# A planned kernel for banded attention and two MLPs: PSUM banks counted per engine, four banks for one block's h, an earlier region, other priorities

## The chip, the cores and the metric

One core of a Trainium2 chip runs the whole program. The metric is the device time of one execution in microseconds; for the kernel before it is the median of three runs. TensorE (PE) does the matrix products and transposes, VectorE (DVE), ScalarE (ACT) and GpSimd (POOL) the elementwise work, SyncE (SP) issues nearly all DMAs. PSUM, where products arrive, has eight banks here, each of 128 partitions by 512 fp32 values.

## What is computed

```python
rel = pos[:, None] - pos[None, :]
mask = (rel >= 0) & (rel < 128)
scores = np.where(mask, q @ k.T / sqrt(64) + slope[head] * -abs(rel), -1e9)
attn = softmax(scores)                       # + 1e-9 in the denominator
x = (attn @ v)                               # 4 x 576 rows = 2304 rows, 8 heads x 64 = 512 columns
h = x @ w_in                                 # 512 -> 2048
P = a[0] + a[1]*h + a[2]*h**2 + a[3]*h**3
Q = 1 + abs(b[0])*abs(h) + abs(b[1])*h**2
x = (P / (Q + 1e-6)) @ w_out                 # 2048 -> 512
h = x @ w2_in                                # the second MLP
out = (h * sigmoid(h)) @ w2_out
```

## The kernel before

Activations lie transposed, features on partitions and rows along the free dimension. Each fp32 factor is split into a high part (rounded to fp32r) and a low part (the rest), and a product is made of three fp32r matmuls: high x high, high x low and low x high.

The 18 tiles of 128 rows form five blocks (4, 4, 3, 4 and 3 tiles, `blk1`). For each block, `group` does attention for the four pairs of heads: scores (L674), a mask and maximum on VectorE (L680, L687), the exponential on ScalarE (L691), normalisation (L710 or L716), transposes (L730), the split of P into own and previous tile (L758, L760 on GpSimd, L767, L771 on VectorE), the product with V (L799) and its high and low parts xh, xl (L811).

`step` does one of the 16 slices of the first MLP's hidden dimension for a block. `mh` makes h in two halves of six matmuls (L844 to L846) in a bank of the pool h, which has two. The rational function follows in eleven operations that alternate between ScalarE (L860, L866, L877, L881, L883) and VectorE (L874, L878, L879, L885, L887, L889), of which L860, L866, L874, L878, L879, L883, L885, L887 and L889 read or write the bank of h; its temporaries t1, t2 and t3 have two buffers each (`actb`). The result's parts gh and gl (`c_hi`, `c_lo`, helpers at L447, L451, L455 for copies and L462, L466 for differences) have three. The second product `ma` (L913 to L915) adds into four banks acc0 to acc3, two and a half steps later. Two more banks, atA and atB, belong to attention, and later to the second MLP.

The second MLP works on thirds of 768 rows, each in phase A and phase B, with seven products in place of eight for a 2 x 2 split (`CHAIN`, Strassen's scheme in Winograd's form). `prep` makes the sums and differences of both weights (raw, sums, st) in DRAM while the first MLP still runs, and the products stream them back. `x_forms` makes seven forms F0 to F6 of a third's input, one buffer each, with differences xs and high and low parts; `phase_a` makes 56 products of six matmuls (L1183 to L1185) and the SiLU (L366); `phase_b` makes 56 chunks of six matmuls (L1249 to L1251), for each of which a high part xh_b and a low part xl_b, and for some a difference g, have to be there first; the rings of xh_b and xl_b hold eight chunks in all. The buffers of the forms lie where attention's lay: `open2` (L1005) closes attention's pools and opens them, and the zero-cost operation `opener` (L1012) waits for the operations in `last_att`.

The order is not written by hand. Each instruction, or bundle, is an `Op` with one or more engines that may run it, a cost in ns, its reads and writes, and a priority in units of a step. `schedule` plays the program once: of all that is ready it takes what can start first, and among those that can start within `look` ns the one with the lowest priority. Ring buffers are handed out in the order of priority. `LATENCY` is added between dependent operations on different engines; `port_free` keeps VectorE and GpSimd apart on SBUF. The order that comes out is the program's order on each engine; the waits on the chip are set by the data and by the banks. `OPT` holds the choices of engine and the leads and distances of priorities (`xlead` of `x_forms`, `hlead` and `tlead` of phase B's operands, `la` and `lb` the lengths of the phases in units, `pw2`, `rw2`, `pwo2`, `rwo2` of `prep`, `pl` of the reload of a partial sum). `SHIFTS` adds an amount to the priorities of runs of operations.

Of the kernel before, what the change touches and what calls it, by code (L numbers as in the profile page):

```python
# [21 lines left out]
P = 128  # L22
# [6 lines left out]
MASK_FAR = 2.56e11  # L29

# [5 lines left out]
    'gh': 'act|dve|pool',  # L36
    'gl': 'pool',
    'whi': 'act',
    'wlo': 'pool',
# [10 lines left out]
    'tabs': 'pool',  # L50
    'stb': 3,
    'strb': 3,
    'wpro': 1.037,
    'dS': -1.576,
    'dT': -0.149,
    'dA': 0.106,
    'dm': 0.288,
    'look': 2.453,
    'pw': -0.828,
    'pwo': -0.969,  # L60
    'dg': 0.261,
# [7 lines left out]
    'pl': 1.625,  # L69
    'qlead': 2.916,  # L70
    'keen': 9999.0,
    'norm0': 'act',
# [6 lines left out]
    'la': 8.923,  # L79
    'lb': 10.6,  # L80
    'dm2': 0.291,
    'sums': 'dve|pool',
    'fhi': 'act|pool',
# [9 lines left out]
    'tlead': 0.985,  # L93
    'hlead': 1.0,
    'oq': 'sp',
    'pw2': 35.931,
    'rw2': 2.459,
    'pwo2': 80.807,
    'rwo2': 0.657,
    'xlead': 7.017,  # L100
    'slead': 1.6,
# [14 lines left out]
]  # L116

def c_act(n, psum=False, aps=0):  # L120
# [1277 lines left out]
```

## Time and profile before

| | |
|---|---|
| median of three runs | 917.33 us (916.65 to 919.83) |
| the profiled execution, its own time | 920.78 us |
| its span, first to last instruction | 918.7 us |
| TensorE busy, share | 875.1 us, 95% |
| VectorE, ScalarE, GpSimd busy, share | 76%, 64%, 67% |
| mean granted clock of TensorE | 0.989 |
| DMA, mean | 249 GB/s, 228.94 MB |

The page gives busy times of one execution. TensorE's busy time contains the time in which a matmul stands in its queue, so the share says little alone; a stretch is read by its count of matmuls beside its length. In a table of stretches, the columns are the stretch, its length, then busy time and, in brackets, the number of instructions of TensorE, its weight loads, VectorE, ScalarE and GpSimd, then the granted clock, the DMA share and GB/s. A timeline row has start and duration in us, engine, line, operation, tile written and tiles read, shape, count, and in square brackets the idle time of the engine before it and what ended that.

### The profile page before, as it was taken

What the parts mean: (1) busy time and instruction counts of PE and PEld (TensorE: products, weight loads), DVE (VectorE), ACT (ScalarE), POOL (GpSimd) and SP (SyncE); (2) the same over time, 40 slices, a digit from 0 to 9 for tenths busy, and PEclk for the clock granted to TensorE, in tenths of its full rate; (3) what the DMA queues carried; (4) which work ended last, traced back from release to release, by engine and by line L of the source; (5) the groups of instructions that cost most, each with busy time, mean ns of one, the idle gap of its engine ahead of it and who ended that gap; (6) DMA issues with size and microseconds to landing.
All of it is one profiled execution on the core that took longest, in us unless ns stands there. A gap on an engine that the chain in (4) does not pass through costs nothing.

```text
span 918.7 us, 15313 instructions
## 1 busy us (share of the span) xinstructions
PE 875.1 (95%) x5072; PEld 769.7 (84%) x5072; DVE 700.7 (76%) x1382; ACT 583.5 (64%) x1253; POOL 618.9 (67%) x591
## 2 busy tenths in 40 slices
PE   8879899999999999999998999999999999999998
PEld 6647667877777888777777989999899998999998
DVE  5789988789999989999998985449843389533662
ACT  5878888689887788878777775336323365233441
POOL 2255655454767779778788776559954499645895
PEclk8989999999999999999999999999999999999999
DMA  7645585367798879757796888988788898788884
GB/s 238 252 133 165 197 273 165 137 199 275 234 340 260 252 243 307 243 192 239 239 345 221 286 266 303 325 296 285 239 279 256 264 307 256 250 270 253 249 269 167
DMA packets 80606, 228.94 MB, mean 249 GB/s; under 512 B 8464, under 2 KB 17168, under 8 KB 80528
## 3 DMA queue, kind: packets, MB, share of 16 engines
q1 hardware_dynamic: 78224, 219.58, 73.3%
q10 hardware_dynamic: 2304, 8.39, 2.3%
q8 instruction: 40, 0.66, 0.3%
q14 instruction: 38, 0.31, 0.1%
HBM read 178.65 MB, written 49.28 MB: 248 GB/s over the span
## 4 chain that ended last, share of the span: by engine, by line
PE 55%; DVE 15%; POOL 10%; ACT 10%; DMA 6%; issue 3%; SPq 0%; POOLq 0%; ACTq 0%; DVEq 0%
PE h L844 4%; PE z_a L1183 4%; PE z_a L1185 4%; PE z_a L1184 4%; PE h L845 3%; PE h L846 3%; POOL xf L466 3%; DVE t L874 3%; PE acc L913 3%; PE acc L915 2%; PE acc L914 2%; ACT t L866 2%; PE z_b L1249 2%; PE z_b L1251 2%; PE z_b L1250 2%
## 5 line engine op out<-in xcount | busy, mean ns | idle before, releaser
L913 PE MATMUL acc<-gh,wo 128*128 128x512 f32 (+1 forms) x320 | 121.4, 379 | 1.0 <-ACT x L447 0.8
L915 PE MATMUL acc<-gl,wo 128*128 128x512 f32 (+1 forms) x320 | 118.3, 370 | 2.7 <-POOL gl L466 2.6
L914 PE MATMUL acc<-gh,wo 128*128 128x512 f32 (+1 forms) x320 | 118.1, 369 | 0.4 <-POOL wo L466 0.4
L447 ACT CAST xh_b<-g 128x384 fp32r<-128x384 f32 x137 | 68.5, 514 | 78.7 <-PE z_b L1251 36.2
L462 DVE TENSOR_TENSOR xl_b<-g,xh_b 128x384 fp32r<-128x384 f32 x75 | 99.3, 1364 | 22.3 <-ACT xh_b L447 19.0
L466 POOL TENSOR_TENSOR gl<-t,gh 128x512 fp32r<-128x512 f32 (+1 forms) x80 | 98.5, 1231 | 22.6 <-ACT gh L447 15.6
L466 POOL TENSOR_TENSOR xl_b<-g,xh_b 128x384 fp32r<-128x384 f32 x93 | 107.6, 1172 | 3.8 <-ACT xh_b L447 1.2
L844 PE MATMUL h<-xh,ws 128*128 128x512 f32 (+1 forms) x256 | 97.0, 379 | 11.3 <-DVE t L889 11.2
L846 PE MATMUL h<-xh,ws 128*128 128x512 f32 (+1 forms) x256 | 93.0, 363 | 0.0
L845 PE MATMUL h<-xl,ws 128*128 128x512 f32 (+1 forms) x256 | 92.9, 363 | 0.0
L366 ACT ACTIVATE g<-t_a 128x384 f32<-128x384 f32 x72 | 37.8, 525 | 84.2 <-DVE t_a L359 84.2
L874 DVE SCALAR_TENSOR_TENSOR t<-t,ab,h 128x512 f32<-128x512 f32 (+1 forms) x80 | 55.3, 691 | 22.6 <-ACT t L866 20.0
L913 PEld LDWEIGHTS acc<-gh,wo 128*128 128x128 f32 x320 | 60.1, 188 | 13.8 <-issue 4.5
L915 PEld LDWEIGHTS acc<-gl,wo 128*128 128x128 f32 x320 | 60.1, 188 | 11.7 <-POOL gl L466 4.1
L844 PEld LDWEIGHTS h<-xh,ws 128*128 128x128 f32 x256 | 48.0, 188 | 25.3 <-DVE t L889 17.9
L466 POOL TENSOR_TENSOR g<-g,g 128x384 f32<-128x384 f32 x57 | 64.6, 1142 | 3.9 <-DVE xl_b L462 1.5
L914 PEld LDWEIGHTS acc<-gh,wo 128*128 128x128 f32 x320 | 60.1, 188 | 8.1 <-POOL wo L466 1.5
L860 ACT ACTIVATE t<-h,ab 128x512 f32<-128x512 f32 (+1 forms) x80 | 51.2, 641 | 23.4 <-PE h L846 22.9
L691 ACT ACTIVATE e<-e,m 128x128 f32<-128x128 f32 x144 | 56.2, 391 | 13.8 <-DVE m L687 13.5
L1183 PE MATMUL z_a<-xf,w2s 128*128 128x384 f32 x192 | 64.2, 334 | 0.4 <-DVE t L889 0.4
L1249 PE MATMUL z_b<-xh_b,wo2s 128*128 128x384 f32 x192 | 64.1, 334 | 0.0
L1251 PE MATMUL z_b<-xh_b,wo2s 128*128 128x384 f32 x192 | 64.1, 334 | 0.0
(178 smaller groups left out, 2736.1 us busy)
## 6 DMA issues: line engine op xcount, KB each, us to landing
w2s<-forms_w SPq DMA_DIRECT2D x84, 512.0 KB, 4.5
wo2s<-forms_wo SPq DMA_DIRECT2D x84, 512.0 KB, 4.6
ws<-sc SPq DMA_DIRECT2D x64, 512.0 KB, 4.8
raw_w<-in_w SPq DMA_DIRECT2D x32, 512.0 KB, 4.9
raw_wo<-in_wo SPq DMA_DIRECT2D x32, 512.0 KB, 4.6
forms_w<-st_w SPq DMA_DIRECT2D x24, 512.0 KB, 5.5
forms_wo<-st_wo SPq DMA_DIRECT2D x24, 512.0 KB, 5.3
sc<-w ACTq DMA_DIRECT2D x16, 512.0 KB, 5.6
```

Of the source, the lines that this page charges most:

```text
L462: nc.vector.tensor_tensor(out=o, in0=a, in1=b, op=op)
L466: nc.gpsimd.tensor_tensor(out=o, in0=a, in1=b, op=op)
L844: nc.tensor.matmul(o, lhsT=T[W][:, 0, c], rhs=xh, start=kt == 0, stop=False)
L845: nc.tensor.matmul(o, lhsT=T[W][:, 0, c], rhs=xl, start=False, stop=False)
L846: nc.tensor.matmul(o, lhsT=T[W][:, 1, c], rhs=xh, start=False, stop=kt == KD - 1)
L874: nc.vector.scalar_tensor_tensor(out=t("t1"), in0=t("t2"), scalar=ab[:, 0:1], in1=hp_(), op0=ALU.add, op1=ALU.mult)
L913: nc.tensor.matmul(a, lhsT=T[WO][:, 0, c], rhs=T[G1][:, :n], start=first_f, stop=False)
L914: nc.tensor.matmul(a, lhsT=T[WO][:, 1, c], rhs=T[G1][:, :n], start=False, stop=False)
L915: nc.tensor.matmul(a, lhsT=T[WO][:, 0, c], rhs=T[G2][:, :n], start=False, stop=last_f)
L1183: nc.tensor.matmul(o, lhsT=w(0, kt * P), rhs=x[:, 0, kt], start=st and kt == 0, stop=False, skip_group_check=True)
L1249: nc.tensor.matmul(o, lhsT=w(0, m * P), rhs=h, start=st and q == 0, stop=False, skip_group_check=True)
L1251: nc.tensor.matmul(o, lhsT=w(1, m * P), rhs=h, start=False, stop=q == NQ - 1, skip_group_check=True)
```

## The change

- `schedule` keeps for each PSUM bank the engine that last used it and when that ends; an operation of another engine on that bank may not start before that end plus the latency. The rule for VectorE and GpSimd on SBUF is kept by engine, with a gap of 60 ns in place of 120. A TensorE operation that starts after an idle time of over 20 ns is counted 110 ns longer, and scores and the product with V 90 ns longer, the first operation on raw weights 45 ns.
- In the last block, steps 2, 3, 6, 7, and so on take the banks atA and atB for h in place of the pool's (`tail`), so four banks go round.
- `last_att` no longer holds the operations on atA and atB.
- More engines are allowed for the parts of g and of the first MLP's weights, the table of biases, block 0's normalisation and the prepared weights' high parts; a ScalarE form of the shift of raw weights is written, and the option leaves it on VectorE. One more constant is set at the start.
- The numbers of `OPT` that set priorities are new, and so is the whole list `SHIFTS`.

```diff
-    'gh': 'act|dve|pool',
-    'gl': 'pool',
-    'whi': 'act',
-    'wlo': 'pool',
+    'gh': 'act|pool',
+    'gl': 'dve|pool',
+    'whi': 'act|pool',
+    'wlo': 'dve|pool',
...
-    'tabs': 'pool',
+    'tabs': 'act|pool',
...
-    'look': 2.453,
+    'look': 3.05,
...
-    'pl': 1.625,
-    'qlead': 2.916,
+    'pl': -6.448,
+    'qlead': 5.608,
...
-    'norm0': 'act',
+    'norm0': 'act|pool',
...
-    'la': 8.923,
-    'lb': 10.6,
-    'dm2': 0.291,
+    'la': 14.638,
+    'lb': 23.993,
+    'dm2': 0.172,
...
-    'fhi': 'act|pool',
+    'fhi': 'act|dve|pool',
...
-    'tlead': 0.985,
-    'hlead': 1.0,
+    'tlead': 1.271,
+    'hlead': -0.51,
...
-    'pw2': 35.931,
-    'rw2': 2.459,
-    'pwo2': 80.807,
-    'rwo2': 0.657,
-    'xlead': 7.017,
-    'slead': 1.6,
+    'pw2': 45.759,
+    'rw2': 6.3,
+    'pwo2': 112.144,
+    'rwo2': 0.672,
+    'xlead': 2.951,
+    'slead': 1.798,
+    'shift': 'dve',
+    'tail': 1,
...
 SHIFTS = [
...
+    (127, 57, -0.49), (282, 5, 1.3), (296, 14, 0.38), (480, 60, 0.03), (676, 69, -0.05), (787, 18, 0.2), (789, 4, -0.96), (919, 10, -0.83),
...
+PORT_GAP = 60.0
+STALL = 110.0
...
-        psum = any(t[0] in ("h", "atA", "atB") or t[0].startswith("acc") for t in list(reads) + list(writes))
-        o.port = {e for e in o.alts if e == "pool" or e == "dve" and not psum}
+        o.banks = {t[:2] for t in list(reads) + list(writes) if t[0] in ("h", "atA", "atB") or t[0].startswith("acc")}
+        o.port = {e for e in o.alts if e == "pool" or e == "dve" and not o.banks}
...
-                when = lambda o: max(f, o.ready, landed[-8] if o.dma and len(landed) >= 8 else 0.0, port_free - 120 if eng in o.port else 0.0)
+                when = lambda o: max([f, o.ready, landed[-8] if o.dma and len(landed) >= 8 else 0.0, port_free["pool" if eng == "dve" else "dve"] - PORT_GAP if eng in o.port else 0.0]
+                                     + [last_in[k][1] + LATENCY[last_in[k][0], eng] for k in o.banks if k in last_in and last_in[k][0] != eng])
...
-                o.end = free[eng] = st + o.cost
+                o.end = free[eng] = st + o.cost + (STALL if eng == "pe" and st > free.get(eng, 0.0) + 20 else 0.0)
                 if eng in o.port:
-                    port_free = o.end
+                    port_free[eng] = o.end
+                for k in o.banks:
+                    last_in[k] = (eng, o.end)
...
-            pl.op(p - 0.5, "dve", c_dve2x(NR), lambda: nc.vector.tensor_scalar(
-                out=low(), in0=low(), scalar1=29, scalar2=None, op0=ALU.logical_shift_right), reads=[rk + (0,)], writes=[rk + (0,)])
+            pl.op(p - 0.5, any_of(OPT["shift"], {
+                "act": (c_act(NR) + 45, lambda: nc.scalar.activation(out=low(), in_=low(), func=AF.Identity, scale=LOW_SCALE, bias=lnb[:, 2:3])),
+                "dve": (c_dve2x(NR), lambda: nc.vector.tensor_scalar(
+                    out=low(), in0=low(), scalar1=29, scalar2=None, op0=ALU.logical_shift_right))}), 0, None, reads=[rk + (0,), ("lnb", 0)], writes=[rk + (0,)])
...
-        Hk = ("h", g)
+        tail = OPT["tail"] and blk == nb1 - 1 and g % 4 > 1
+        Hk = (("atA", "atB")[g % 2], f"h{g}") if tail else ("h", g)
...
-                T[Hk] = h_p.tile([P, 512], F32, tag="h", name=f"h{g}")
+                T[Hk] = banks[Hk[0]] if tail else h_p.tile([P, 512], F32, tag="h", name=f"h{g}")
...
-    last_att = [o for k, l in pl.tile_ops.items() if k[0] in ("kd", "qd", "vh", "e", "ph", "m", "l", "atA", "atB", "tab", "tabs") for o in l]
+    last_att = [o for k, l in pl.tile_ops.items() if k[0] in ("kd", "qd", "vh", "e", "ph", "m", "l", "tab", "tabs") for o in l]
```

## Rows read from the trace of the kernel before

**Rows 1.** busy time, share and instructions of each engine, from the page

```profile
PE 875.1 (95%) x5072; PEld 769.7 (84%) x5072; DVE 700.7 (76%) x1382; ACT 583.5 (64%) x1253; POOL 618.9 (67%) x591
```

**Rows 2.** stretches: length, busy us and instructions by engine, clock, DMA share

```profile
35.70:471.90 436.20, 414.63 (x2413) 323.62 (x2409) 396.77 (x911) 351.14 (x768) 285.76 (x275) 0.99 0.71 233
...
471.90:551.00 79.10, 71.28 (x385) 66.44 (x385) 70.11 (x122) 61.75 (x114) 63.73 (x65) 1.00 0.81 271
...
504.90:546.20 41.30, 39.19 (x217) 37.24 (x217) 36.29 (x68) 32.77 (x62) 30.15 (x37) 1.00 0.86 281
...
612.80:676.10 63.30, 61.07 (x341) 60.10 (x340) 51.88 (x45) 30.52 (x61) 60.04 (x43) 0.97 0.84 273
676.10:733.90 57.80, 57.80 (x336) 57.80 (x335) 22.17 (x40) 18.82 (x38) 26.40 (x30) 1.00 0.83 264
```

**Rows 3.** timeline of TensorE at 469 us: start, duration, line, tiles

```profile
468.88 0.39 PE L846 MATMUL h<-xh,ws 128*128 128x512 f32 x1
469.11 0.39 PE L913 MATMUL acc<-gh,wo 128*128 128x512 f32 x1
```

**Rows 4.** waits of TensorE in the whole span: total us, times, longest

```profile
PE h L844 <- DVE t L889: 14.9, 20, 2.1
PE bank_atA L799 <- POOL ph L760: 5.3, 2, 3.2
```

**Rows 5.** waits of TensorE in 471.9:551, and who waits for L889 later

```profile
PE h L844 <- DVE t L889: 5.4, 8, 2.1
PE acc L915 <- POOL gl L466: 2.0, 1, 2.0
...
  PE z_a L1183: 0.4, 1
```

**Rows 6.** timeline in the last block, one wait and one step's h and t3

```profile
519.01 0.45 PE L844 MATMUL h<-xh,ws 128*128 128x384 f32 x1 [0.98 <-DVE t L889]
...
521.93 0.67 ACT L866 ACTIVATE t<-h,na 128x384 f32<-128x384 f32 x1
...
527.30 0.55 DVE L889 SCALAR_TENSOR_TENSOR t<-t,h 128x384 f32<-128x384 f32 x1
...
528.47 1.02 POOL L466 TENSOR_TENSOR gl<-t,gh 128x384 fp32r<-128x384 f32 x1
```

**Rows 7.** waits of VectorE in 35.7:471.9: total us, times, longest

```profile
DVE t L874 <- ACT t L866: 15.8, 28, 1.1
```

**Rows 8.** tiles w and st_wo: duration of one in ns, least, median, most

```profile
L466 POOL TENSOR_TENSOR w<-raw_w,w x16: 1290/1311/1774, 27.6 to 214.8; 128x512 fp32r<-128x512 f32 x16
...
L462 DVE TENSOR_TENSOR st_wo<-sums_wo,st_wo x4: 692/920/1490, 449.9 to 565.3; 128x512 fp32r<-128x512 f32 x4
```

**Rows 9.** groups in 612.8:676.1: count, busy us, mean ns, idle time before

```profile
L462 DVE TENSOR_TENSOR xl_b<-g,xh_b 128x384 fp32r<-128x384 f32 x28 | 38.4, 1413 | 7.8 <-ACT xh_b L447 7.8
L466 POOL TENSOR_TENSOR xl_b<-g,xh_b 128x384 fp32r<-128x384 f32 x20 | 25.7, 1305 | 0.7 <-ACT xh_b L447 0.6
...
L466 POOL TENSOR_TENSOR g<-g,g 128x384 f32<-128x384 f32 x12 | 14.2, 1196 | 0.6 <-DVE xl_b L462 0.5
...
L466 POOL TENSOR_TENSOR xf<-xf 128x768 fp32r<-128x768 f32 x3 | 6.3, 2117 | 0.1
```

**Rows 10.** timelines of GpSimd and TensorE near 660 us

```profile
656.38 2.15 POOL L466 TENSOR_TENSOR xf<-xs,xf 128x768 fp32r<-128x768 f32 x1
...
660.25 0.69 PE L1250 MATMUL bank_atA<-xl_b,wo2s 128*128 128x384 f32 x1 [2.02 <-POOL xl_b L466]
...
661.05 0.52 PE L1249 MATMUL bank_atB<-xh_b,wo2s 128*128 128x384 f32 x1
661.37 0.52 PE L1250 MATMUL bank_atB<-xl_b,wo2s 128*128 128x384 f32 x1
```

**Rows 11.** tile xl_b: duration of one in ns, least, median, most

```profile
L466 POOL TENSOR_TENSOR xl_b<-g,xh_b x93: 1004/1027/1732, 556.4 to 908.1; 128x384 fp32r<-128x384 f32 x93
L462 DVE TENSOR_TENSOR xl_b<-g,xh_b x75: 545/1364/2249, 614.7 to 901.4; 128x384 fp32r<-128x384 f32 x75
```

More of the change, by code (lines that the diff above doesn't have):

```diff
@@ L29 @@
 MASK_FAR = 2.56e11
+LOW_SCALE = 2.0 ** -29 * (1.0 - 2.0 ** -21)
 OPT = {
@@ L49 @@
     'vb': 3,
-    'tabs': 'pool',
+    'tabs': 'act|pool',
     'stb': 3,
     'strb': 3,
[L53 to L57, printed above, removed]
-    'look': 2.453,
-    'pw': -0.828,
-    'pwo': -0.969,
-    'dg': 0.261,
+    'wpro': 0.411,
+    'dS': -1.564,
+    'dT': -0.234,
+    'dA': 0.111,
+    'dm': 0.297,
+    'look': 3.05,
+    'pw': -0.803,
+    'pwo': -1.106,
+    'dg': -0.074,
     'lead': 2.526,
@@ L154 @@
 class Op:
-    __slots__ = ("eng", "cost", "fn", "alts", "prio", "deps", "ndep", "users", "start", "end", "allocs", "ready", "idx", "after", "port", "dma")
+    __slots__ = ("eng", "cost", "fn", "alts", "prio", "deps", "ndep", "users", "start", "end", "allocs", "ready", "idx", "after", "port", "dma", "banks")
 class Plan:
@@ L232, in schedule @@
         free = {}
-        port_free = 0.0
+        port_free = {"dve": 0.0, "pool": 0.0}
+        last_in = {}
         dma_free, landed = 0.0, []
@@ L477, in plan_kernel @@
         ab = const.tile([P, 2], F32, name="ab")
-        lnb = const.tile([P, 2], F32, name="lnb")
+        lnb = const.tile([P, 3], F32, name="lnb")
         tabs = tab_p.tile([P, H, 4, P], F32, name="tabs")
@@ L484, in k_ident @@
         nc.vector.memset(lnb[:, 1:2], -LN2_63)
+        nc.vector.memset(lnb[:, 2:3], 2.0 ** -18 - 0.5)
     pl.op(-99, "pool", 600, k_ident, writes=[("ident", 0), ("lnb", 0)])
@@ L540, in raw_weight @@
             low = lambda: T[rk][:, :, 0].bitcast(U32)
-            pl.op(p - 0.6, "act", c_act(NR), lambda: nc.scalar.activation(out=top(), in_=top(), func=AF.Prelu, scale=2.0 ** -112, alpha=2.0 ** 32),
+            pl.op(p - 0.6, "act", c_act(NR) + 45, lambda: nc.scalar.activation(out=top(), in_=top(), func=AF.Prelu, scale=2.0 ** -112, alpha=2.0 ** 32),
                   reads=[rk + (1,)], writes=[rk + (1,)])
-            pl.op(p - 0.5, "dve", c_dve2x(NR), lambda: nc.vector.tensor_scalar(
-                out=low(), in0=low(), scalar1=29, scalar2=None, op0=ALU.logical_shift_right), reads=[rk + (0,)], writes=[rk + (0,)])
+            pl.op(p - 0.5, any_of(OPT["shift"], {
+                "act": (c_act(NR) + 45, lambda: nc.scalar.activation(out=low(), in_=low(), func=AF.Identity, scale=LOW_SCALE, bias=lnb[:, 2:3])),
+                "dve": (c_dve2x(NR), lambda: nc.vector.tensor_scalar(
+                    out=low(), in0=low(), scalar1=29, scalar2=None, op0=ALU.logical_shift_right))}), 0, None, reads=[rk + (0,), ("lnb", 0)], writes=[rk + (0,)])
             pl.op(p - 0.3, "dve", c_dve(NR), lambda: nc.vector.scalar_tensor_tensor(
@@ L675, in s_mm @@
                                              start=True, stop=True)
-            pl.op(pH, "pe", 120 + sum(c_pe4(P if k0[i] else 192) for i in half), s_mm, reads=[("kd", gi), ("qd", gi)], writes=list(S_))
+            pl.op(pH, "pe", 210 + sum(c_pe4(P if k0[i] else 192) for i in half), s_mm, reads=[("kd", gi), ("qd", gi)], writes=list(S_))
             if two:
@@ L799, in av @@
                     nc.tensor.matmul(T[AV][r, cs_], lhsT=v[:, iv, r], rhs=rhs(hh), start=k == 0, stop=k == len(steps) - 1)
-        pl.op(pA, "pe", 200 + (n + sum(1 - k for k in k0)) * 215, av, reads=[("vh", gi), PH], writes=[AV])
+        pl.op(pA, "pe", 290 + (n + sum(1 - k for k in k0)) * 215, av, reads=[("vh", gi), PH], writes=[AV])
         XH, XL = (f"xh{hp}", f"1_{bi}"), (f"xl{hp}", f"1_{bi}")
```

11 rows, old and new, of the table SHIFTS are left out of this document.

## The prediction

> **What bounds the kernel now.** I read the page's busy lines first: TensorE is busy 875.1 of a span of 918.7 us [rows 1]. A queue of matmuls counts as busy while it crawls, so I then read the table of stretches, which holds the number of matmuls beside each stretch's length [rows 2], and priced the matmuls at the rate they have when nothing disturbs them. In 676.10:733.90 there are 336 matmuls of 384 columns in 57.8 us, 0.172 us each; matmuls of 512 columns start 0.23 us apart [rows 3]. That gives each stretch a floor.
>
> - Last block of the first MLP, 471.90:551.00: 385 matmuls, of which 25 still have 512 columns (they belong to the block before): 360 x 0.172 + 25 x 0.23 = 67.7 us against 79.1. Excess 11.4 us.
> - Second MLP, phase B of the first third, 612.80:676.10: 341 x 0.172 = 58.7 us against 63.3. Excess 4.6 us. The second third's phase B is the same again; the last third has no forms to make for a successor. Phase A is at its floor.
> - The rest of the first MLP with attention, 35.70:471.90: 436.2 us, in which VectorE is busy 396.8, ScalarE 351.1 and GpSimd 285.8 [rows 2]. TensorE's work there mixes attention's small matmuls with the MLP's, so I take no floor but the waits: 5.3 us for attention's split P on GpSimd, in two places, and for L889, VectorE's last operation on h, 14.9 us in the whole span [rows 4], of which 5.4 belong to the last block [rows 5]: 9.5 before it.
>
> So the kernel is bound by TensorE in phase A, by VectorE and TensorE together before 471.90, and by a chain on the h bank in the last block.
>
> **The change part by part. Sums are made against the profiled execution, 920.78 us (span 918.7 and 2.1 around it), which lies 3.45 us above the median of the runs, 917.33; a saving is taken off the median.**
>
> *Four banks for the last block's h.* Before 519.01 TensorE stands for 0.98 us, and what it waits for is VectorE's L889 [rows 6]. L889 is the last reader of the h bank of two steps before, and h has two banks. The bank's round goes from the first matmul into it (519.01) to the end of its L889 (527.30 + 0.55 = 527.85), 8.84 us, and two banks give one step per 4.42 us. Measured are nine steps in 504.90:546.20, 4.59 us each [rows 2], against 24 x 0.172 = 4.13. With four banks the bank gives a step per 2.2 us and is out of the way. What is late next is t3, which has two buffers: L866 takes one at 521.93, and it is free when the low part gl is done, 528.47 + 1.02 = 529.49 [rows 6]: 7.56 us, or 3.78 per step. That is just under TensorE's 4.13, so TensorE becomes the bound, with 0.35 us a step to spare. TensorE's waits for L889 in this block sum to 5.4 us in 8 places, and 2.0 us is one wait for gl that no bank shortens [rows 5]. The nine regular steps can give 9 x 0.46 = 4.1 us, the first seven up to 11.4 - 4.1 - 2.0 = 5.3. I take 5.5 us of the 9.4, somewhat over half, because the regular steps are the surer part; bounds 0 (t3 binds instead) and 9.4.
>
> *The region of the second MLP's operands opens sooner.* It no longer waits for attention's last reads of atA and atB, which now are also banks of h. TensorE's first product of phase A waits for L889, 0.4 us [rows 5], not for an operand, so this is worth nothing; bounds 0 and 0.4. The last block's 79 us lie over it; without that cover it would be worth one more read of a bank, which I bound by a VectorE operation of 0.55 us [rows 6].
>
> *The schedule knows that a bank belongs to one engine at a time.* The chip's program already does: VectorE's L874 needs only L860's output, yet starts after ScalarE's L866 on the same bank, 28 times in 35.70:471.90 with 15.8 us of VectorE's idle time [rows 7]. No instruction goes away. What changes is that the planner's due times agree with what happens, so an order that looked free and cost a wait is avoided. Its price can't be read; it is in the next item.
>
> *New priorities and wider choices of engine before 471.90.* The low parts of the weights and of g may now go to VectorE as well: 32 of w and wo and 80 of gl, 112 in all. On GpSimd a 512-wide one takes 1.31 us, on VectorE between 0.69 and 1.49, median 0.92 [rows 8]. VectorE has 436.2 - 396.8 = 39.4 us idle, GpSimd 150.4. The planner gives a piece to whichever can start first; split like the idle time, VectorE gets 39.4 / 189.8 = 21%, 23 pieces, 21 us. That fits into its idle time, while 23 x 1.31 = 30 us leave GpSimd. High parts of g lose VectorE, and those of w may go to GpSimd, which has room: I cost both at nothing, since GpSimd's idle 150 us hide them; without that cover each is an operation of about the low part's price. The waits of TensorE there sum to 9.5 + 5.3 = 14.8 us [rows 4]; new due times may save some. I take 6 us, nearer to the middle of these than to either end, since VectorE is busy 91% and can't shift much; bounds -15 (VectorE is overloaded, below) and +15 (all of them go).
>
> *The x forms of the next third.* In 612.80:676.10 48 low parts xl_b, one for every 1.03 us of TensorE, and 17 differences g (12 of them on GpSimd) are made on VectorE and GpSimd; in the same stretch GpSimd makes forms xf and differences xs of 2.1 us each, 9 of them (three stand in [rows 9]), 18.9 us. GpSimd is busy 60.0 of 63.3 us. Before 660.25 TensorE stands for 2.0 us for an xl_b on GpSimd, and then runs at half clock until about 663.5: starts 0.32 us apart instead of 0.17, nine of them, 1.4 us [rows 10]. But these forms are needed only at 676.10, some 17 us after GpSimd is done with them (656.38 + 2.15 [rows 10]), and in phase A VectorE and GpSimd are busy 22.2 and 26.4 of 57.8 us [rows 2]. The old xlead of 7.0 of a phase B of 10.6 units puts them 34 to 71% into phase B; the new 2.95 of 24.0 puts them from 88% on, behind nearly all low parts. So I expect the low parts on time and the forms in the last 10 us and in phase A's first products. Of twice 4.6 us I take 4, a little under half: the forms' work stays, and only what phase A can take of it is won; bounds -9 (the stall moves to phase A and doubles) and +9.
>
> *Small edits.* One more memset before the first load has landed; the shift stays on VectorE; the changed costs alter no instruction. Nothing.
>
> Sum: 5.5 + 0 + 6 + 4 = 15.5 us. 917.33 - 15.5 = 901.8, rounded to 902. All bounds at once would be 884 (9.4 + 0.4 + 15 + 9 saved) and 941 (15 + 9 lost).
>
> **A rule weighed.** The trace has xl_b on VectorE at 545, 1364 and 2249 ns (least, median, most), on GpSimd at 1004, 1027 and 1732 [rows 11]: VectorE waits inside the instruction while GpSimd works. The Trainium skill, SBUF — State Buffer, section Terms, calls the pair of ports that the two share an exclusive lock, held for the whole instruction, so that the loser blocks. By that rule alone the choice between the two engines, which this change widens, gives nothing. The trace agrees in part: on VectorE the median is 2.5 times the least.
>
> **The rivals.**
> - *Turns on VectorE and GpSimd.* If the two only take turns, 28 xl_b at 0.545 and 20 at 1.0, 12 g at 1.0 and 5 at 0.55, 9 forms at 2.1 on GpSimd and 2 at 0.9 on VectorE make 15.3 + 20 + 12 + 2.8 + 18.9 + 1.8 = 70.8 us in a stretch of 63.3 [rows 9, 11]. As it is done in 63.3, some overlaps, but the excess of phase B can't be ordered away. Then 4 us are missing: 906. Chance 0.10.
> - *The stall moves to phase A.* If half of the forms (11 x 2.1 / 2 = 11.5 us, on two engines 5.8) are pending at phase A's first product, and the clock falls as at 660 (1.4), each third loses 7.2 us instead of 4.6: minus 5.2 instead of plus 4, so 911. For it: the new lead is 12% of phase B, about 7 us, against 23 us of work. Against it: products need the seven forms one by one, 1.03 us apart. Chance 0.10.
> - *Nothing on the path.* The h bank is replaced by t3 (0.35 us of room only), and VectorE, 91% busy, sets the pace before 471.90 whatever the order: 1 or 2 us in all, 916. Chance 0.14.
> - *Slower: VectorE is overloaded.* Place: 35.70:471.90. Price: each low part on VectorE is 0.92 us of its time. Of 39.4 us idle, 15.8 are waits inside the chain of a step [rows 7], which a low part can't always use: 23.6 to 39.4 are free. So it decides from 26 to 43 pieces of 112. At half of them, 51.5 us, 12 to 28 are over; with 20 of them on the path, the 6 not gained and the other two terms kept, 917.3 - 9.5 + 20 = 928. For it: a piece started at the wrong time delays the chain even when there is room. Against it: GpSimd is idle four times as long. Chance 0.14.
>
> **How the numbers follow.** The forecast has 0.52; its own range is 886 to 911. About 0.3%, 2.8 us, is what a measurement of this kernel can tell from no change: faster is below 914.6, slower above 920.1. Faster: 0.52 + 0.10 + 0.10 and a little of the third rival, 0.02: 0.74. Same: the rest of that rival, 0.12. Slower: 0.14. The range leaves out the lowest end of the forecast, 0.07, and of the overload all but its beginning, 0.12: 885 to 922.
>
> **What would show it.** In the last block: waits of h for L889 near zero, nine steps at 4.2 us, 24 x 0.172 between equal matmuls of two steps; if t3 binds, ScalarE's L866 waits for gl instead. At the end of phase B: no wait for xl_b, clock 1.0, forms close to phase A or within it; if the stall moved, waits of the first products of phase A for xf. Before 471.90: a count of gl, w and wo on VectorE under 40, and the first product of the last block before 466 us. The prediction is wrong if VectorE's busy time before the last block grows by more than 30 us, if the last block keeps 79 us, or if the phases gain while 0:167 loses.

## The result, and the profile after

The changed kernel takes 892.89 us (median of four runs, 890.19 to 896.57) against 918.58 for the kernel before beside it (four runs, 916.65 to 921.41): a ratio of 0.972, 95% interval 0.967 to 0.977. Forecast were 902, 885 to 922. So the direction was right and the time lies in the range, but the saving is 25.7 us where 15.5 were worked out. The profiled execution of after has 896.57 us, of which 894.8 are its span.

The lines moved by a few: L889 is now L896, L874 is L881, L866 is L873, L760 is L766; among the helpers L447 is L450, L462 is L465, L466 is L469; phase A's products are L1190 to L1192, phase B's L1256 to L1258.

TensorE's share of busy time rises from 95 to 97% (864.4 of 894.8 us on after's page, [rows 1]).

The table of stretches of after (stretch, length, busy us and instructions of TensorE, its weight loads, VectorE, ScalarE, GpSimd, granted clock, DMA share, GB/s): everything from the first h to the last block, the last block, phase A, phase B and the next phase A, and a regular part of the last block (from the second half of its fifth h to the start of its fifteenth):

```profile
35.50:463.00 427.50, 411.55 (x2388) 324.95 (x2385) 393.27 (x906) 343.21 (x740) 284.86 (x281) 0.98 0.71 240
463.00:536.30 73.30, 69.73 (x386) 66.61 (x386) 69.66 (x121) 60.39 (x115) 62.01 (x63) 1.00 0.81 276
536.30:599.00 62.70, 62.15 (x356) 61.26 (x356) 33.90 (x56) 26.27 (x52) 36.28 (x41) 1.00 0.91 305
599.00:657.70 58.70, 58.70 (x340) 58.70 (x339) 48.34 (x46) 31.54 (x61) 56.70 (x42) 1.00 0.88 294
657.70:715.40 57.70, 57.70 (x334) 57.70 (x334) 22.39 (x41) 18.64 (x38) 28.45 (x31) 1.00 0.83 267
...
485.51:527.26 41.75, 41.27 (x235) 40.40 (x235) 39.88 (x74) 33.06 (x64) 32.05 (x37) 1.00 0.88 296
```

Beside [rows 2]: up to the last block 436.2 has become 427.5 (8.7 us less), the last block with the phase A behind it 140.9 (471.9 to 612.8) has become 136.0 (4.9 less; the two are taken together, since matmuls of one overlap the other), phase B 63.3 has become 58.7. From 612.8 (after: 599.0) the two phases B and the A between them fell from 184.9 to 175.3 us, 9.6 less. Those three are 23.2 of the 23.9 us that the spans differ by. Phase B is now at the floor of the prediction, 341 x 0.172 = 58.7, with TensorE busy in all of it.

TensorE's waits in after, in the last block (first two rows) and before it (us in all, times, longest):

```profile
PE h L851 <- DVE t L896: 1.9, 1, 1.9
PE acc L922 <- POOL gl L469: 1.7, 3, 0.8
...
PE h L851 <- DVE t L896: 4.9, 8, 1.7
PE bank_atA L805 <- POOL ph L766: 1.6, 1, 1.6
```

In the last block the 5.4 us in 8 places [rows 5] are one wait of 1.9, early in it; gl, which no bank shortens, is still there. Before it, 9.5 us for the h bank have become 4.9, and 5.3 for the split P 1.6. Other waits of TensorE there have grown, those for attention's operations on VectorE above all; all that the view lists sum to 15.7 us, before to 21.1. In 599:720 no wait of TensorE is listed.

Phase B's groups in 599:657.7 (count, busy us, mean ns, idle time before and what ended it) and the tile xl_b over the whole span (least, median, most ns):

```profile
L465 DVE TENSOR_TENSOR xl_b<-g,xh_b 128x384 fp32r<-128x384 f32 x31 | 36.6, 1201 | 7.1 <-ACT xh_b L450 7.0
L469 POOL TENSOR_TENSOR xl_b<-g,xh_b 128x384 fp32r<-128x384 f32 x17 | 22.3, 1329 | 0.5 <-ACT xh_b L450 0.4
L469 POOL TENSOR_TENSOR g<-g,g 128x384 f32<-128x384 f32 x15 | 18.3, 1236 | 0.6 <-DVE xl_b L465 0.5
...
L469 POOL TENSOR_TENSOR xl_b<-g,xh_b x84: 1003/1031/1779, 542.2 to 883.6; 128x384 fp32r<-128x384 f32 x84
L465 DVE TENSOR_TENSOR xl_b<-g,xh_b x84: 558/1104/2199, 554.4 to 883.7; 128x384 fp32r<-128x384 f32 x84
```

The count of low parts is the same 48 as before [rows 9]; only who makes them (31 and 17 in place of 28 and 20) and when has changed. GpSimd's timeline (start, us, line, tiles) before, from the longest run of forms:

```profile
649.25 1.83 POOL L466 TENSOR_TENSOR xf<-xs,xf 128x768 fp32r<-128x768 f32 x1
651.16 2.04 POOL L466 TENSOR_TENSOR xs<-xf,xf 128x768 f32<-128x768 f32 x1
653.16 1.14 POOL L455 TENSOR_SCALAR xf<-xf 128x768 fp32r<-128x768 f32 x1
654.39 2.03 POOL L466 TENSOR_TENSOR xf<-xf 128x768 fp32r<-128x768 f32 x1
```

and after, the first form operation and the end of phase B, with TensorE's first product of the phase A that follows:

```profile
626.88 2.17 POOL L469 TENSOR_TENSOR xs<-xf,xf 128x768 f32<-128x768 f32 x1
...
645.93 2.15 POOL L469 TENSOR_TENSOR xs<-xf,xs 128x768 f32<-128x768 f32 x1
648.05 1.85 POOL L469 TENSOR_TENSOR xf<-xs,xf 128x768 fp32r<-128x768 f32 x1
649.97 2.05 POOL L469 TENSOR_TENSOR xs<-xf,xf 128x768 f32<-128x768 f32 x1
651.99 3.01 POOL L469 TENSOR_TENSOR xl_b<-g,xh_b 128x384 fp32r<-128x384 f32 x2
654.97 2.16 POOL L469 TENSOR_TENSOR xf<-xf 128x768 fp32r<-128x768 f32 x1
657.09 2.56 POOL L469 TENSOR_TENSOR xf<-xs,xf 128x768 fp32r<-128x768 f32 x1
...
657.71 0.33 PE L1190 MATMUL z_a<-xf,w2s 128*128 128x384 f32 x1
```

Before, GpSimd made five form operations in a row from 649.25 to 658.5, of which [rows 10] hold the last, with no low part between them, and was done 17 us before phase A. Now at most three stand in a row (645.93 to 652.0), low parts stand between the others, and the last form ends at 659.65, 1.94 us into phase A. The first form starts 28 us into phase B (626.88), before 10 us (622.7); so the forms run through the second half of the phase, between the low parts, and not only at its end.

### The profile page after: what moved, and what is told of

The parts are those of the page before. It is cut to its first block, busy times and chain, and to the rows that moved or that the text cites. A ratio compares the mean times of both kernels' runs of the same rounds, so it can differ in the third digit from the quotient of the medians.

```text
span 894.8 us, 15273 instructions
## 1 busy us (share of the span) xinstructions
PE 864.4 (97%) x5052; PEld 766.5 (86%) x5052; DVE 688.5 (77%) x1395; ACT 577.3 (65%) x1230; POOL 610.0 (68%) x590
## 4 chain that ended last, share of the span: by engine, by line
PE 72%; DVE 11%; DMA 5%; ACT 4%; POOL 4%; issue 2%; SPq 0%; ACTq 0%; POOLq 0%; DVEq 0%
PE acc L920 4%; PE h L851 4%; PE acc L922 4%; PE acc L921 4%; PE h L853 4%; PE h L852 4%; PE z_b L1258 4%; PE z_b L1256 4%; PE z_b L1257 4%; PE z_a L1190 4%; PE z_a L1192 4%; PE z_a L1191 4%; DMA raw_wo<-in_wo 4%; PE bank_atA L805 2%; PE bank_atA L680 2%
## 5 line engine op out<-in xcount | busy, mean ns | idle before, releaser
L450 ACT CAST xh_b<-g 128x384 fp32r<-128x384 f32 x139 | 71.2, 514 | 67.5 <-PE z_b L1258 45.8
L465 DVE TENSOR_TENSOR xl_b<-g,xh_b 128x384 fp32r<-128x384 f32 x84 | 90.0, 1082 | 26.9 <-ACT xh_b L450 26.4
L469 POOL TENSOR_TENSOR gl<-t,gh 128x512 fp32r<-128x512 f32 (+1 forms) x72 | 89.8, 1247 | 25.2 <-ACT gh L450 23.1
L469 POOL TENSOR_TENSOR xl_b<-g,xh_b 128x384 fp32r<-128x384 f32 x84 | 98.2, 1175 | 7.2 <-ACT xh_b L450 4.8
L851 PE MATMUL h<-xh,ws 128*128 128x512 f32 (+1 forms) x224 | 84.8, 379 | 3.6 <-DVE t L896 3.6
L853 PE MATMUL h<-xh,ws 128*128 128x512 f32 (+1 forms) x224 | 82.2, 367 | 0.0
L852 PE MATMUL h<-xl,ws 128*128 128x512 f32 (+1 forms) x224 | 82.2, 367 | 0.0
L469 POOL TENSOR_TENSOR g<-g,g 128x384 f32<-128x384 f32 x63 | 72.8, 1164 | 5.9 <-ACT g L369 2.6
L1190 PE MATMUL z_a<-xf,w2s 128*128 128x384 f32 x192 | 64.3, 335 | 0.0
L1191 PE MATMUL z_a<-xf,w2s 128*128 128x384 f32 x192 | 64.1, 334 | 0.0
L1192 PE MATMUL z_a<-xf,w2s 128*128 128x384 f32 x192 | 64.1, 334 | 0.0
L1256 PE MATMUL z_b<-xh_b,wo2s 128*128 128x384 f32 x192 | 64.1, 334 | 0.0
L1257 PE MATMUL z_b<-xl_b,wo2s 128*128 128x384 f32 x192 | 64.1, 334 | 0.0
L1258 PE MATMUL z_b<-xh_b,wo2s 128*128 128x384 f32 x192 | 64.1, 334 | 0.0
```

The lines of the kernel that those rows point to most:

```text
L469: nc.gpsimd.tensor_tensor(out=o, in0=a, in1=b, op=op)
L851: nc.tensor.matmul(o, lhsT=T[W][:, 0, c], rhs=xh, start=kt == 0, stop=False)
L852: nc.tensor.matmul(o, lhsT=T[W][:, 0, c], rhs=xl, start=False, stop=False)
L853: nc.tensor.matmul(o, lhsT=T[W][:, 1, c], rhs=xh, start=False, stop=kt == KD - 1)
L1190: nc.tensor.matmul(o, lhsT=w(0, kt * P), rhs=x[:, 0, kt], start=st and kt == 0, stop=False, skip_group_check=True)
L1191: nc.tensor.matmul(o, lhsT=w(0, kt * P), rhs=x[:, 1, kt], start=False, stop=False, skip_group_check=True)
```

## The experiments

Each was timed beside runs of the kernel before on its own chip, so times are compared by their ratios to it; 0.01 is 9.2 us. Stage lengths are read from one profile of each, as above. How far one profile can be trusted is seen where kernels have the same order of instructions: from the first h to the last block the changed kernel and experiments 2, 4 and 12 take 427.5, 424.7, 424.8 and 427.8 us, the kernel before and experiments 1 and 3 take 436.2, 435.9 and 440.2, experiments 6 and 9 take 439.6 and 443.7. A difference under 4 us in that stretch is therefore not read as an effect.

**1. The four banks alone, in the kernel before.**

```diff
-        Hk = ("h", g)
+        tail = blk == nb1 - 1 and g % 4 > 1
+        Hk = (("atA", "atB")[g % 2], f"h{g}") if tail else ("h", g)
...
-    last_att = [... "m", "l", "atA", "atB", "tab", "tabs") ...]
+    last_att = [... "m", "l", "tab", "tabs") ...]
```

> The kernel before with four banks for the last block's h alone (the region's opening with it, which the banks need). If the bank is what the last block waited for: the last block falls from 79.1 us to about 74, TensorE's waits for L889 in it from 5.4 us to under 2.5, and the time by 4 to 6 us, to about 913. If t3 or VectorE binds in its place: under 1.5 us in all, and ScalarE's L866 waits for gl instead.

Measured: 915.12, ratio 0.994 (0.991 to 0.996). Last block and phase A of this kernel, and TensorE's waits in the last block (its lines from 830 on are one above those of before: L890 is L889):

```profile
467.70:543.50 75.80, 69.49 (x374) 64.35 (x373) 68.92 (x117) 57.26 (x108) 58.73 (x59) 1.00 0.75 260
543.50:607.40 63.90, 63.90 (x368) 63.37 (x367) 33.68 (x59) 28.85 (x58) 39.09 (x45) 1.00 0.89 315
...
PE acc L916 <- POOL gl L466: 4.1, 7, 1.6
PE acc L914 <- POOL gh L455: 1.0, 2, 0.6
PE h L845 <- DVE t L890: 0.6, 1, 0.6
```

75.8 + 63.9 = 139.7 us against 140.9: 1.2 us. The wait for the bank is nearly gone (5.4 to 0.6), but waits for gl and gh on GpSimd take its place (5.1 us in 9 places, before 2.0 in 1). The sign that was named for t3, ScalarE's L866 waiting for gl, is weak: 0.8 us in 2 places, before 0.4 in 1. In the old order of priorities the banks only change what is late. The two profiles' spans differ by 6.4 us, of which 3.9 are an earlier start (first h at 31.8 us) and 1.2 the banks' stage; whether the start is earlier in every run isn't shown, as only one run of each was profiled.

**2. The changed kernel with two banks for h.**

```diff
-    'tail': 1,
+    'tail': 0,
```

> The changed kernel with two banks for the last block's h. If the banks made the last block's 5.8 us: it goes back from 73.3 us to about 79, and the time rises by 5 to 6 us, to about 898.5. If the new due times did it and not the banks: under 2 us, about 894.

Measured: 896.07, ratio 0.974 (0.971 to 0.976). Last block, phase A, and the wait for the bank:

```profile
457.40:529.90 72.50, 67.95 (x361) 63.86 (x360) 68.19 (x117) 59.11 (x111) 57.98 (x59) 0.98 0.79 275
529.90:596.80 66.90, 66.46 (x381) 65.40 (x380) 36.73 (x63) 30.23 (x61) 33.98 (x38) 1.00 0.86 295
...
PE h L851 <- DVE t L896: 4.6, 7, 1.9
```

139.4 us against 136.0, and the wait is back (4.6 us in 7 places): in the new order the banks give 3.4 us by the stages. The whole time shows 0.0015 of 918.6, 1.4 us, with intervals that overlap. So by the stages some 3.4 of the 4.9 us in the last block are the banks', and about 1.5 the other priorities'; experiments 4, 11 and 12, which keep the four banks, have about 136 us there, as after has.

**3. The forms late, in the kernel before:** the new numbers of the second MLP alone.

```diff
-    'la': 8.923, 'lb': 10.6, 'dm2': 0.291, 'tlead': 0.985, 'hlead': 1.0, 'slead': 1.6,
+    'la': 14.638, 'lb': 23.993, 'dm2': 0.172, 'tlead': 1.271, 'hlead': -0.51, 'slead': 1.798,
...
-        F = x_forms(g, baseA[g] - OPT["xlead"])
+        F = x_forms(g, baseA[g] - (OPT["xlead"] if g == 0 else 2.951))
```

> The kernel before with the second MLP's distances and leads of the changed kernel (la, lb, dm2, tlead, hlead, slead, and xlead from the second third on). If the place of the x forms behind the low parts is what phase B lost: phases B of the first and second third fall from 63.3 and 63.9 us to about 59, no wait for xl_b at their end, clock 1.0 there, time lower by 8 to 10 us, about 909. If the new account of the port and of the banks is needed too: the waits stay or move to phase A, within 3 us of the kernel before.

Measured: 923.57, ratio 1.004 (1.001 to 1.007). Phase B did not shrink. Its stretch; TensorE's first matmul after the longest stand; GpSimd's difference xs, VectorE's form and the add v behind it; and v at the same place before:

```profile
621.10:685.80 64.70, 60.53 (x341) 60.24 (x340) 53.57 (x47) 30.80 (x60) 57.42 (x42) 0.97 0.79 267
...
676.36 0.66 PE L1249 MATMUL bank_atA<-xh_b,wo2s 128*128 128x384 f32 x1 [4.17 <-issue]
...
671.91 2.12 POOL L466 TENSOR_TENSOR xs<-xf,xf 128x768 f32<-128x768 f32 x1
...
674.06 1.73 DVE L462 TENSOR_TENSOR xf<-xf 128x768 fp32r<-128x768 f32 x1 [1.69 <-POOL xs L466]
675.72 0.54 DVE L1269 TENSOR_TENSOR v<-v,bank_atA 128x384 f32<-128x384 f32 x1
```

```profile
667.60 0.55 DVE L1269 TENSOR_TENSOR v<-v,bank_atA 128x384 f32<-128x384 f32 x1 [1.20 <-PE bank_atA L1251]
```

The wait for xl_b has gone, and TensorE stands for 4.17 us at 676.36. "issue" in the row only says that no semaphore event explains the stand; the order of the operations does. The product at 676.36 adds on to a sum in bank atA that VectorE's v has to read first. The products up to that reading ended at 671.7, but v runs only at 675.72 to 676.26: ahead of it VectorE's program has a form's low part, which waits 1.69 us for GpSimd's xs, and that xs stands behind three low parts. TensorE starts 0.10 us after v ends. Before, v starts within 0.1 us of the end of the products that it reads, and TensorE's next product on that bank also starts 0.10 us after v (668.26). The second phase B shows the same: v ends at 798.69, TensorE starts at 798.79 after 4.15 us. The expectation of experiment 9 names another cause, weights loaded behind a store on SP; but the last of those loads was issued by 668.38, and none in this stretch takes over 5.4 us to land, so all were there by 673.8. So late forms are not enough: pushed behind the low parts, they get in the way of v. This profile (930.98 us) is one of the longest of the ten runs (918 to 931), and 8.1 us of its excess lie in the last block, which this edit doesn't touch and where the planned order is as before.

**4. The forms early, in the changed kernel.**

```diff
-        F = x_forms(g, baseA[g] - OPT["xlead"])
+        F = x_forms(g, baseA[g] - (OPT["xlead"] if g == 0 else 15.9))
```

> The changed kernel with the x forms of the second and third third at 34% of phase B, as before (xlead 15.9 of 24.0 units), all else the same. If their place is the cause: each of the two phases B grows by 4 to 5 us, with a wait of about 2 us for xl_b and a stretch at half clock, time higher by 8 to 10 us, about 902. If the rest of the second MLP's priorities did it: within 2 us of the changed kernel, about 893.

Measured: 910.3, ratio 0.989 (0.987 to 0.992): 16 us lost. Phase B, TensorE's waits in it, and GpSimd ahead of the longest of them:

```profile
594.70:663.30 68.60, 62.42 (x342) 61.39 (x341) 50.29 (x47) 31.09 (x60) 55.82 (x42) 0.95 0.75 250
...
PE bank_atA L1257 <- POOL xl_b L469: 3.7, 1, 3.7
...
625.40 4.22 POOL L469 TENSOR_TENSOR xf<-xs,xf 128x768 fp32r<-128x768 f32 x2
629.59 7.06 POOL L469 TENSOR_TENSOR xl_b<-g,xh_b 128x384 fp32r<-128x384 f32 x6
```

The old wait is back, and larger: a low part stands behind two forms, and its product starts at 630.94 after 3.72 us. 15.9 units of 24.0 put the first form, by its priority, where the old numbers had it, 34% into the phase. But the spacing of the forms is in units too, so here they are made within 24 us (605.2 to 629.6), before within 37 (622.7 to 659.4). The run shows that the place and the spacing of this work decide; the size of the loss, 9.9 us in the first phase B, isn't that of the kernel before.

**5. The changed kernel without the account of banks.**

```diff
-                                     + [last_in[k][1] + LATENCY[last_in[k][0], eng] for k in o.banks if k in last_in and last_in[k][0] != eng])
+                                     + [])
```

> The changed kernel whose schedule doesn't count a bank as taken by one engine; priorities, shifts and engines stay. If the rule itself is worth the 8.9 us gained before the last block: that stretch goes back from 463.0 to about 472 us and the time rises to about 902 or more. If only the numbers that were fitted to it matter: as the order changes from the first 50 us on, a rise of similar size is possible for that reason too; a rise under 3 us would show that the rule is worth little. VectorE's waits for L866 then sum to the same or more.

Measured: 902.75, ratio 0.982 (0.980 to 0.984): 9 us lost. Phase B, with VectorE's wait of L881 before the last block; then the same wait in after:

```profile
601.00:663.90 62.90, 60.21 (x340) 58.46 (x339) 48.58 (x44) 30.16 (x61) 60.03 (x44) 1.00 0.82 291
...
DVE t L881 <- ACT t L873: 14.0, 26, 1.5
```

```profile
DVE t L881 <- ACT t L873: 7.4, 14, 1.3
```

With the account, the wait of L881 behind ScalarE on the same bank halves (14.0 in 26 places to 7.4 in 14; before 15.8 in 28 [rows 7]). TensorE hardly gains by that: its waits in this stretch sum to 15.5 us without the account and 15.7 with it, and the two that the prediction named (L896 and ph L766) to 1.7 and 6.5. In the profiles the loss is 1.5 us up to the last block, 2.4 in the last block and phase A (138.4 against 136.0) and 4.2 in the first phase B, while the second phase B (58.8 us) loses nothing. What is left without the account is still a gain of 16.6 us over the kernel before.

**6. The new account alone, in the kernel before:** banks, the rule for VectorE and GpSimd by engine, the counted stall and three costs, with the old numbers and engines.

```diff
+PORT_GAP = 60.0
+STALL = 110.0
...
-                when = lambda o: max(f, o.ready, ..., port_free - 120 if eng in o.port else 0.0)
+                when = lambda o: max([f, o.ready, ..., port_free["pool" if eng == "dve" else "dve"] - PORT_GAP if eng in o.port else 0.0]
+                                     + [last_in[k][1] + LATENCY[last_in[k][0], eng] for k in o.banks if k in last_in and last_in[k][0] != eng])
```

> The kernel before, its priorities, shifts and engines, under the new account of banks, port and stalls. If a truer account makes a better order by itself: faster than before by 5 us or more, the stretch before the last block under 467 us. If the priorities were fitted to the old account and lose their fit: same or slower, 917 to 930.

Measured: 919.74, ratio 1.002 (0.999 to 1.004). Up to the last block, and the first phase B with the phase A behind it:

```profile
36.00:475.60 439.60, 415.73 (x2413) 326.53 (x2410) 401.33 (x915) 352.85 (x767) 284.83 (x274) 0.98 0.68 231
...
618.90:675.70 56.80, 55.98 (x320) 55.05 (x319) 46.28 (x44) 30.18 (x59) 53.98 (x40) 1.00 0.86 286
675.70:737.10 61.40, 61.40 (x357) 61.40 (x356) 24.40 (x43) 19.88 (x41) 29.61 (x33) 1.00 0.81 267
```

The pair of phases (their products overlap at the border, so they are added) takes 118.2 us against 121.1 (63.3 + 57.8): 6 us won over two pairs, though the numbers of the second MLP are the old ones. 3.4 us are lost up to the last block, which kernels of one order differ by as well, and 2.4 in the last block with phase A. In sum nothing.

**7, 8. The changed kernel with the old choices of engine for the parts of g and of the first MLP's weights; and without its list of shifts.**

```diff
-    'gh': 'act|pool', 'gl': 'dve|pool', 'whi': 'act|pool', 'wlo': 'dve|pool',
+    'gh': 'act|dve|pool', 'gl': 'pool', 'whi': 'act', 'wlo': 'pool',
```

> The changed kernel with the old choices of engine for the parts of g and of the first MLP's weights (low parts on GpSimd alone, high parts of the weights on ScalarE alone). If the wider choice is worth part of the gain before the last block (22 high parts of 32 moved off ScalarE, 13 low parts onto VectorE): slower by 3 to 8 us, all before 463 us. If the choice is worth nothing: within 2 us of the changed kernel, about 893.

```diff
-SHIFTS = [ ... ]
+SHIFTS = []
```

> The changed kernel without its list of shifts. If the single shifts carry the gain before the last block: slower by 8 us or more, with waits spread over the first MLP. If the account and the leads carry it: slower by less than 4 us, about 896.

Measured: 891.62, ratio 0.970 (0.967 to 0.972), and 895.71, ratio 0.974 (0.970 to 0.977). Up to the last block, of 7 and of 8:

```profile
33.40:457.00 423.60, 407.93 (x2389) 322.41 (x2386) 389.48 (x899) 346.63 (x746) 284.92 (x278) 1.00 0.71 241
...
35.20:459.90 424.70, 408.58 (x2373) 324.16 (x2370) 393.87 (x900) 337.96 (x729) 288.15 (x285) 0.99 0.69 235
```

Neither can be told from the changed kernel. With the old engines, the stretch in which the prediction wanted VectorE's help isn't longer (423.6 against 427.5). These choices of engine and the shifts carry nothing that these runs can measure; the other wider choices (`tabs`, `norm0`, `fhi`) were not taken back.

**9. Account and late forms together, in the kernel before:** the edits of 3 and 6.

> The kernel before under the new account (as in e6) and with the second MLP's distances and leads of the changed kernel (as in e3). In e3 the late forms removed the waits for xl_b, but TensorE stood 4.2 us at a chunk whose weights were loaded behind a store of the output on SyncE's queue. If the account is what puts that store and the weights in the right order: phases B and A between the first B and the last A fall from e6's 56.8 + 61.4 us to 58.7 + 57.7 each, no wait over 1 us there, time 3 to 4 us under e6, about 916. If the two don't add up: the weights' wait of 4 us is there again, 923.

Measured: 917.79, ratio 0.998 (0.995 to 1.001). Phase B:

```profile
620.30:679.70 59.40, 58.94 (x340) 58.65 (x339) 45.71 (x46) 31.53 (x61) 56.72 (x42) 1.00 0.87 289
```

59.4 + 57.8 = 117.2 us for the pair: 121.1 before, 118.2 with the account alone, 116.4 in the changed kernel. TensorE's stand of experiment 3 is nearly gone (0.9 us in 2 places, one in each phase B): v now starts within 0.4 us of the end of the products that it reads. What is won here, about 8 us over two pairs, is lost in the first MLP: from the first h, at 33.9, to the last block, at 477.6, it takes 443.7 us against 436.2, of which 4.1 are a difference from experiment 6 with the same order there.

**10, 11. The changed kernel with the old leads of attention and the first MLP; and with the old leads of the preparation of weights.**

```diff
-    'wpro': 0.411, 'dS': -1.564, 'dT': -0.234, 'dA': 0.111, 'dm': 0.297, 'look': 3.05, 'pw': -0.803, 'pwo': -1.106, 'dg': -0.074, 'pl': -6.448, 'qlead': 5.608,
+    'wpro': 1.037, 'dS': -1.576, 'dT': -0.149, 'dA': 0.106, 'dm': 0.288, 'look': 2.453, 'pw': -0.828, 'pwo': -0.969, 'dg': 0.261, 'pl': 1.625, 'qlead': 2.916,
```

> The changed kernel with the old numbers for the first MLP and attention (wpro, dS, dT, dA, dm, pw, pwo, dg, pl, qlead, look). If these leads made the gain before the last block (8.9 us in the profiles, up to 11.4 by e4, which has the same order there): 35 to 460 us becomes about 436 us again instead of 425 to 427.5 and the time rises by 8 to 11 us, to 902. If the account of the banks carries it: under 4 us, about 896.

```diff
-    'pw2': 45.759, 'rw2': 6.3, 'pwo2': 112.144, 'rwo2': 0.672,
+    'pw2': 35.931, 'rw2': 2.459, 'pwo2': 80.807, 'rwo2': 0.657,
```

> The changed kernel with the old places for the preparation of the second MLP's weights (pw2, rw2, pwo2, rwo2). If moving it back behind the steps is part of the gain: blocks 3 to 5 (steps 32 to 79) longer by 3 us or more together, time about 897. If it fills idle time at either place: within 2 us of the changed kernel.

Measured: 898.61, ratio 0.978 (0.975 to 0.981), and 894.29, ratio 0.973 (0.970 to 0.976). Of 10, the stretch up to the last block and TensorE's two largest waits in it:

```profile
32.00:468.20 436.20, 416.65 (x2413) 327.27 (x2409) 400.51 (x920) 337.59 (x735) 291.29 (x294) 0.98 0.68 233
...
PE h L851 <- DVE t L896: 7.1, 12, 1.8
PE bank_atA L805 <- POOL ph L766: 3.8, 1, 3.8
```

With the old leads the stretch is the 436.2 us of before, to the tenth, and the two waits make 10.9 us, between the 14.8 of before and the 6.5 of after. All listed waits of TensorE make 19.3 us, between the 21.1 of before and the 15.7 of after. So the leads carry the gain up to the last block; 5.5 us of it are left in the whole time (0.006 of 918.6, with intervals that overlap a little), since the last block is shorter here (133.6 us with phase A). The place of the preparation costs nothing that the time shows; only the first phase B is longer in its profile, 61.0 us, and there TensorE waits 0.7 us for a v that stands behind two forms, the stand of experiment 3 in small.

**12. The changed kernel, with the region again waiting for attention's reads of atA and atB.**

```diff
-"m", "l", "tab", "tabs") for o in l]
+"m", "l", "tab", "tabs") or k[0] in ("atA", "atB") and k[1][0] != "h" for o in l]
```

> The changed kernel whose region of the second MLP's operands opens only after attention's operations on atA and atB, as before (the tail's use of these banks left out of the wait). The prediction's value for the earlier opening is 0 (0 to 0.4 us): within 2 us of the changed kernel. If the forms of the first third, loaded earlier, matter to the last block: 2 us or more slower, all between 463 and 599 us.

Measured: 893.98, ratio 0.974 (0.971 to 0.976). Last block and phase A:

```profile
463.00:533.90 70.90, 67.87 (x373) 64.62 (x374) 65.30 (x116) 58.68 (x109) 52.56 (x50) 1.00 0.77 269
533.90:599.00 65.10, 64.17 (x367) 63.30 (x366) 37.72 (x63) 30.70 (x62) 40.02 (x46) 1.00 0.91 319
```

70.9 + 65.1 = 136.0, as in after. The earlier opening is worth nothing.

## Why the prediction was right, and where it was not

*Four banks, 5.5 us: right size, partly another's work.* The stage gained 4.9. The working holds nearly: the regular part of the block has 234 products in 41.75 us, 4.28 for the 24 of a step, where 4.13 to 4.2 were forecast and 4.59 measured before; TensorE waits once in it, 0.5 us for gl. ScalarE's L873 now waits for gl (1.8 us in 4 places, before 0.4 in 1), the sign named for t3. But the next in the chain was taken too lightly: in the old order gl and gh come late to TensorE, and only 1.2 us come out (experiment 1). The lower bound of that term, "0 (t3 binds instead)", was nearly true there, though by gl and gh more than by t3; with the new order it is 3.4 (experiment 2).

*Region, 0: right* (experiment 12). The reason given, that the last block covers it, was not tested by itself.

*Up to the last block, 6 us: 8.7 measured, sign right, cause half wrong.* The term was argued from low parts that VectorE takes over from GpSimd. By the tiles of after, VectorE took 13 of 112 (8 gl, four of them in the last block, and 5 of w and wo; under the 40 that were named, and under the 23 worked out), and its busy time fell from 396.8 to 393.3. That step was worth nothing (experiment 7). What the term also named, due times that save waits, came true: with the old leads of attention and the first MLP the stretch is 436.2 us again (experiment 10). The two waits that were named fell from 14.8 to 6.5 us, all of TensorE's listed ones by 5.4; where the other 3.3 of the 8.7 us went isn't shown. The account of banks is not behind it: without it the stretch takes 429.0 us and TensorE waits as little (experiment 5). The last block's first product was to come before 466 us; it came at 463.0.

*The x forms, 4 us: 9.6 measured. This is the term that was mis-sized.* The floor was read rightly (4.6 us of excess twice), and so was the wait. The step that failed is "the forms' work stays, and only what phase A can take of it is won". It took GpSimd's 60.0 busy us of 63.3 for a lack of capacity. The same 48 low parts, and forms that reach only 1.94 us into phase A, fit into 58.7 us, now that low parts stand between the forms and not behind a run of five. The excess was order, with the split of the low parts over the two engines that goes with it, and not capacity. The place of the forms was also misread: it was taken from their priorities, 88% into the phase, but a priority only decides between operations that are ready, and GpSimd starts the first form nearly half way through (28 of 58.7 us). Nor did the new lead alone do it, as the prediction had it: alone it moved the stall to VectorE's v, behind a form (experiment 3, +2 us); the account alone gave 6 of the 9.6 (experiment 6), both 8 (experiment 9). Which of the new account's rules does it in phase B was only tried for the banks, 4.2 us in the first phase B and none in the second (experiment 5); the rule for VectorE and GpSimd was not tried by itself.

*The rivals.* "Turns on VectorE and GpSimd" falls. By the least times in after, 31 and 17 xl_b at 0.558 and 1.003, 15 g at 1.0, eight form operations of about 2.0 on GpSimd and three on VectorE at the prediction's 0.9 are some 68 us, now in 58.7. The Trainium skill's lock in SBUF — State Buffer, section Terms, held for a whole instruction, would not let that fit, if the least times are what is held. The trace agrees with it in part: in this stretch both engines' xl_b are longer than their least, 1201 ns in the mean against 558 on VectorE and 1329 against 1003 on GpSimd. "The stall moves to phase A" did not come: no wait in 599:720; in experiment 3 a stall moved, but to v inside phase B, which no rival had. "Nothing on the path" was nearly right for experiment 1, not for the whole. "VectorE is overloaded" falls with the 13 pieces, half of the number from which it decides.

*The range.* The own range of the forecast, 886 to 911, held. The mid-value missed 10.2 us: 5.6 of it are the forms and 2.7 the stretch up to the last block; the banks are 0.6 the other way, the start and the last third give 0.7, and the rest, 1.8, is the difference between the spans (23.9) and the medians (25.7). That the total lies in the range is partly luck: two of its three terms came out by other work than the one they were argued from.

*What stays open.* The parts don't add: account and late forms without the new leads give nothing in time (experiment 9), old leads with all else give 20 us (experiment 10). The account with the old leads gives nothing (experiment 6), while the new leads without the account of banks keep 16.6 of the 25.7 us (experiment 5). That each set of leads fits the account that it was set against is one reading of this, argued and not shown; the new leads in the kernel before, under its whole old account, were not run.

## What to carry to other kernels

Where an engine is nearly full over a stretch but the stretch is above the floor of the one it feeds, look at the order of its work before calling it capacity: who could have waited, and by how much. Then look at what the moved work now stands in front of: in experiment 3 it was one add that frees a bank. A buffer that is added shows only if the next operations in the chain (here gl and gh) are given time by the order too. And a better model in the planner can give nothing by itself while the priorities stay the old ones (experiment 6), so the two are best changed and judged together.

## What was not expected of the hardware

- Kernels whose first instructions are the same or nearly so begin their first h anywhere from 31.8 us (experiment 1) to 36.0 (experiment 6); in after TensorE waits 2.8 us there for the first load, in experiment 2 0.7. That is larger than several effects looked for here, so stretches were compared from the first h on.
- The mean granted clock is 0.93 of 2.4 GHz over the first 16 steps of after, where TensorE is busy 118.0 of 128.9 us, and 1.00 in each later stretch shown. Before, it is 0.97 there. The order of instructions isn't what decides it: experiments 2, 4 and 12 have the order of after in these steps, at 0.96, 0.96 and 0.92. No part of the change was aimed at this, and experiment 10, with the old leads, has 0.93 there as well.
- Kernels with nearly the same instructions spread differently: experiment 3 from 918 to 931 us in ten runs, experiment 5 from 901.9 to 902.8 in four.
